# Decoding both weights in turn, with 512 tokens instead of 256 taken through float32 at the start of a fused attention and expert kernel

## The chip, the cores and the metric

The kernel runs on one core of one Trainium2 chip. The metric is the device time of one execution in microseconds (us), the median of several runs. The engines are TensorE (PE, matmuls; PEld is its weight load), VectorE (DVE), ScalarE (ACT), GpSimd (POOL) and SyncE (SP, which issues most DMAs, in program order).

## What is computed

Eight batches of 512 tokens and 32 state rows, 512 features in 8 heads of 64, go through an attention between tokens and states in both directions; the 4608 resulting rows go through a dense squared-ReLU layer (2048 wide), and then through 8 experts (1024 wide), of which each row takes one.

```python
scores = scale * x @ state.T ; a = softmax(scores) ; xread = a @ state
scores2 = scale * state @ x.T ; a2 = softmax(scores2) ; sread = a2 @ x
x = concat([xread, sread])            # 4608 rows of 512
g = relu(x @ w_in) ** 2 ; y = g @ w_out
e = argmax(cos(y, expert_emb))        # one expert a row
out = gate * (relu(y @ w1[e]) @ w2[e])
```

The two weights w_in (512x2048) and w_out (2048x512) arrive as float64; the kernel has to make float32 out of their bits before it can use them. The error allowed is small, so a product in 16 bits is made as three float16 matmuls (high by high, high by low, low by high halves); a float32 product needs no split.

## The kernel before, in words

**Order of the work.** The kernel is one program, written out by a small list scheduler in Python (`Plan`, lines 97 to 167): each piece of work is a generator that yields the engine and the estimated time that it wants next; the scheduler lets the piece go first that can start earliest, and of several with the same start the one with the lower priority number. What comes out is a fixed order of instructions on each engine. Priorities stand at the top (`PRIO_WI` and so on) and where threads are added (lines 1691 to 1707).

**Weights.** Each weight is 8 blocks of 1 MB of float64 (256 columns of w_in, or 256 rows of w_out). `block` (line 725) asks for a block into a raw place, `to_f32` (line 738) decodes it: one ACT instruction (line 759), then DVE lines 762, 764 and 775, each over 128x1024. `wi_scale` (786) takes the largest column norm of a w_in block: ACT square (792), four matmuls (799), a DVE reduction (803) and four tiny DVE instructions. `wi_block` (810) then splits the decoded block into float16 halves `wi_h` (ACT, 818) and `wi_l` (DVE, `split_lo`, line 305). All of w_in comes first, then w_out: `wo_square` (827) squares a block on ACT, and after the eighth `weights` (853) makes the scale of w_out and `wo_split` (876) splits its blocks (ACT 885, DVE 305).

**Attention.** `attention` (432) takes batch b: sums of squares on ACT (444), scales on DVE, then the products of state and tokens (625, 495), a softmax, and two transposing DMAs into `aT` (533). `state_side` (608) does the other direction; it ends in matmuls 667 to 669. `state_w` (540) multiplies the batch's state by w_in, in four parts k of 512 columns, each of 24 small float16 matmuls (561, 64 rows by 32 columns, in two row groups and four column groups), and splits the result into `sw` (ACT 566, DVE 305). So the first product of the dense layer is done as (attention weights) x (state x w_in).

**Dense layer.** `up1` (1188) goes over units u of 256 tokens, 17 in all, and over 8 chunks c of 256 hidden columns: 12 matmuls each (1210 to 1212), then `hidden` (1155) on ACT and DVE: ReLU (1166), square, and a split into `g_h`, `g_l`. For u = 0 the square is kept in float32 (`g32`, 1170); for u = 1 both the high half (1177) and the square (1179) are made on ACT; for later u DVE casts (1182). DVE subtracts (1184). `down1` (1227) multiplies by w_out: for u = 0 in float32 straight from the decoded blocks (1272, two tiles of 128 tokens side by side, 8 steps q), for u >= 1 in float16, 96 matmuls a unit (1294 to 1296). `up1` for u >= 2 waits for the down product of unit u-2, and chunk by chunk for that of u-1. `route_tile` (1030) takes each finished tile of 128 rows out of PSUM (two such places, `d_slots`): ACT square (1037), four tiny DVE instructions, ACT (310) and DVE (305) split; for the tiles of u = 0 it first waits for the scale of w_out.

**Experts.** `experts` (909) rewrites the 32 MB of expert weights as scaled float16 halves, in the gaps that ACT and DVE have beside the dense layer: squares (963), then splits into `he`, written back by DMA. It uses three places for raw halves until the attention is over. When it is done, SP loads each expert's weights (1510) and the second half of the kernel starts (`up2`, line 1586, matmuls 1604 to 1606; `down2`, 1629).

## Time and profile before

| | |
|---|---|
| median of 3 runs | 1111.26 us (1108.6 to 1115.41) |
| the profiled execution's own time | 1114.48 us |
| its span, first to last instruction | 1112.6 us |
| TensorE busy | 1030.8 us (93%) |
| DVE, ACT busy | 702.4 us (63%), 575.4 us (52%) |
| mean granted TensorE clock | 0.977 |

A window row gives, for a stretch of the span, how long each engine was busy in it and (in brackets) how many instructions that were, then the granted TensorE clock as a share of 2.4 GHz, the busy share of the DMA engines and their GB/s. A timeline row gives start, duration, engine, line, operation, what it writes and reads, sizes, and how many alike were merged. A matmul's duration includes its way through the array; back-to-back matmuls start closer together than that. A row of groups gives count, busy time, mean ns of one, and the idle time before them with what ended it.

### The profile page before, as it was taken

What the parts mean: (1) busy time and instruction counts of PE and PEld (TensorE: products, weight loads), DVE (VectorE), ACT (ScalarE), POOL (GpSimd) and SP (SyncE); (2) the same over time, 40 slices, a digit from 0 to 9 for tenths busy, and PEclk for the clock granted to TensorE, in tenths of its full rate; (3) what the DMA queues carried; (4) which work ended last, traced back from release to release, by engine and by line L of the source; (5) the groups of instructions that cost most, each with busy time, mean ns of one, the idle gap of its engine ahead of it and who ended that gap; (6) DMA issues with size and microseconds to landing.
All of it is one profiled execution on the core that took longest, in us unless ns stands there. A gap on an engine that the chain in (4) does not pass through costs nothing. (4 is left out here: it accounts for less than half of the span.)

```text
span 1112.6 us, 26342 instructions
## 1 busy us (share of the span) xinstructions
PE 1030.8 (93%) x10655; PEld 666.7 (60%) x10655; DVE 702.4 (63%) x1831; ACT 575.4 (52%) x949; POOL 128.7 (12%) x149
## 2 busy tenths in 40 slices
PE   3279789999999999999999999899999999999998
PEld 2135456555556565555555666477776767777674
DVE  6997788868888869897698777365322223222222
ACT  5678977786878777677777676210111101011110
POOL 0200000200201002001001020312121211212101
PEclk9589999999999999999999999999999999999999
DMA  8546354783668746766658487962796776594691
GB/s 291 193 156 208 100 130 123 208 219 110 169 197 186 221 150 157 216 164 189 209 115 250 132 258 222 345 140 70 250 293 155 208 227 206 159 295 135 179 299 78
DMA packets 160543, 211.74 MB, mean 190 GB/s; under 512 B 112225, under 2 KB 113505, under 8 KB 155170
## 3 DMA queue, kind: packets, MB, share of 16 engines
q1 hardware_dynamic: 152098, 182.94, 57.2%
q0 software_dynamic: 8320, 27.08, 7.7%
q8 instruction: 85, 1.39, 0.5%
q14 instruction: 40, 0.33, 0.1%
HBM read 257.92 MB, written 51.68 MB: 278 GB/s over the span
## 5 line engine op out<-in xcount | busy, mean ns | idle before, releaser
L1560 ACT ACTIVATE r<-u 128x512 f32<-128x512 f32 x70 | 41.8, 597 | 332.6 <-PE u L1606 322.0
L1294 PE MATMUL d<-wo_t,g 128*128 128x512 f16 x512 | 194.3, 380 | 3.2 <-DVE rec L305 1.9
L1296 PE MATMUL d<-wo_t,g 128*128 128x512 f16 x512 | 194.1, 379 | 0.7 <-DVE g L1184 0.6
L1295 PE MATMUL d<-wo_t,g 128*128 128x512 f16 x512 | 194.2, 379 | 0.0
L1210 PE MATMUL u<-aT,sw 128*128 128x256 f16 x512 | 140.6, 275 | 16.6 <-ACT r L1166 13.8
L1212 PE MATMUL u<-aT,sw 128*128 128x256 f16 x512 | 140.4, 274 | 0.0
L1211 PE MATMUL u<-aT,sw 128*128 128x256 f16 x512 | 140.3, 274 | 0.0
L1563 DVE CAST hh<-r 128x512 f16<-128x512 f32 x70 | 29.9, 427 | 141.8 <-ACT r L1560 140.3
L1166 ACT ACTIVATE r<-u,cg 128x512 f32<-128x512 f32 x128 | 87.2, 683 | 58.5 <-PE u L1212 36.5
L1139 POOL DMA_INDIRECT rec_d<-rec,pi x34 | 38.9, 1143 | 564.8 <-DVE g L1184 145.8
L1574 DVE TENSOR_SCALAR o<-d,rec,wo_t 128x512 f32<-128x512 f32 x35 | 28.3, 810 | 106.6 <-PE d L1629 103.1
L1184 DVE TENSOR_TENSOR g<-r,g 128x512 f16<-128x512 f32 x128 | 87.6, 687 | 1.8 <-ACT r L1179 0.4
L1629 PEld LDWEIGHTS <-hh 128*128 128x128 f16 (+1 forms) x688 | 54.5, 102 | 56.5 <-issue 0.4
L1296 PEld LDWEIGHTS <-g 128*128 128x128 f16 x512 | 50.1, 98 | 62.2 <-DVE g L1184 2.3
L1294 PEld LDWEIGHTS <-g 128*128 128x128 f16 x512 | 50.3, 98 | 50.7 <-DVE g L1182 2.3
L1179 ACT ACTIVATE r<-r 128x512 f32<-128x512 f32 x128 | 79.9, 627 | 1.5
L1295 PEld LDWEIGHTS <-g 128*128 128x128 f16 x512 | 50.1, 98 | 49.3 <-issue 2.3
L1604 PE MATMUL u<-xes,stage 128*128 128x128 f16 x448 | 78.0, 222 | 0.7 <-issue 0.7
L1605 PE MATMUL u<-xes,stage 128*128 128x128 f16 x448 | 78.0, 222 | 0.0
L1606 PE MATMUL u<-xes,stage 128*128 128x128 f16 x448 | 78.0, 222 | 0.0
L1604 PE MATMUL u<-xes,xx 128*128 128x128 f16 x416 | 70.6, 219 | 0.5 <-DMA xes<-rec 0.5
L1606 PE MATMUL u<-xes,xx 128*128 128x128 f16 x416 | 70.5, 219 | 0.0
(334 smaller groups left out, 2609.0 us busy)
## 6 DMA issues: line engine op xcount, KB each, us to landing
w_d<-he SPq DMA_DIRECT2D x128, 256.0 KB
g<-w_d SPq DMA_DIRECT2D x16, 2048.0 KB
wo_t<-w_d SPq DMA_DIRECT2D x16, 2048.0 KB
stage<-w_d SPq DMA_DIRECT2D x14, 2048.0 KB
he<-w_d SPq DMA_DIRECT2D x14, 2048.0 KB
xx<-w_d SPq DMA_DIRECT2D x13, 2048.0 KB
sw<-w_d SPq DMA_DIRECT2D x13, 2048.0 KB
stage<-in_w_dram SPq DMA_DIRECT2D x20, 1024.0 KB
```

What stands on the lines that cost most here:

```text
L1166: nc.scalar.activation(out=r, in_=ps, func=AF.Relu, scale=cg[:, g:g + 1] if u else cgq[:, c:c + 1])
L1179: nc.scalar.activation(out=r, in_=r, func=AF.Square)
L1184: V.tensor_tensor(out=gl, in0=r, in1=gh, op=ALU.subtract)
L1210: mm(o, lhsT=hl[:, i, 0, fs], rhs=aT[:, i, :], start=i == 0, stop=False)
L1211: mm(o, lhsT=hl[:, i, 0, fs], rhs=aT[:, 2 + i, :], start=False, stop=False)
L1212: mm(o, lhsT=hl[:, i, 1, fs], rhs=aT[:, i, :], start=False, stop=i == 1)
L1294: mm(ps, lhsT=g_h[:, f, ts], rhs=w[:, 0, :], start=f == 0, stop=False)
L1295: mm(ps, lhsT=g_h[:, f, ts], rhs=w[:, 1, :], start=False, stop=False)
L1296: mm(ps, lhsT=g_l[:, f, ts], rhs=w[:, 0, :], start=False, stop=f == KF - 1)
L1604: mm(p[:, j, xs], lhsT=w[:, 0, k, fs], rhs=xe[:, k, xs], start=k == 0, stop=False)
L1605: mm(p[:, j, xs], lhsT=w[:, 0, k, fs], rhs=xe[:, 4 + k, xs], start=False, stop=False)
L1606: mm(p[:, j, xs], lhsT=w[:, 1, k, fs], rhs=xe[:, k, xs], start=False, stop=k == 3)
```

## The change

- The blocks come in the order of `BLOCKS`: two of w_in, two of w_out, in turn, instead of all of w_in first. Raw places are named per block (`RAW_IN`); eight blocks have a free place at once, and the other eight take turns in four places, each freed when the block in it has been decoded and squared (`freed`).
- Decoded w_in lies in float32 (`wi32`) in the place of the next block's halves (w_in's halves are one tile `wi_t` now), and is split later (`wi_split`, priority 1.3), in order, after the float32 product has read it.
- Batch 0's state product (`first_state_w`) is made in float32 from `wi32`, eight matmuls of 256 columns for each block, as soon as two blocks of w_in are decoded; the scale of each block is put on when the result is split into `sw`. The scale of w_in is computed for two blocks at a time.
- `F32U = 2`: units u = 0 and u = 1 (512 tokens, four tiles) go through w_out in float32. Their chunks of `up1` alternate by k; `down1` does u = 0, all q, then u = 1, all q. The tiles of both wait in `route_tile` for the scale of w_out. w_out is split (priority 1.6 instead of 0.5) after the last w_in split, and block q after u = 1's product has read block q-2.
- `hidden` for u >= 2 lets ACT make the high half where DVE's planned queue is longer than ACT's by over 1 us (`Plan.load`), otherwise DVE.
- Expert halves have two raw places at first, a third (`third`) when w_out is split; fetching of experts waits for the last raw blocks and no longer for the split of w_out.
- The loader of tokens waits for block 9 of the new order instead of block 11 of the old; `group_unscale` waits for the scale of w_out; `switch` has priority 2.1 instead of 2.5.

```diff
+BLOCKS = [(kind, 2 * k + i) for k in range(NB // 2) for kind in "io" for i in range(2)]
+RAW_IN = ('g0', 'g2', 'stage0', 'stage1', 'g1', 'g3', 'phl', 'wo8', 'stage0', 'stage1', 'phl', 'wo8', 'stage0', 'stage1',
+          'phl', 'stage0')
+F32U = 2
+PRIO_SPLIT = 1.3
...
+    def load(self, eng):
+        waiting = [r for th in self.threads if isinstance(r := th[3], tuple) and r[0] == eng and th[2] <= self.free[eng]]
+        return self.free[eng] + sum(r[1] for r in waiting)
...
+    wi32 = [(wi_t[:, q + 1].rearrange("p h k f -> p (h k f)") if q < NB - 1 else
+             wo[0].rearrange("p a k d -> p (a k d)")).bitcast(F32).rearrange("p (k f) -> p k f", k=4) for q in range(NB)]
...
+    def first_state_w(stf):
+        at = plan.now()
+        for k in range(4):
+            yield sw_slots
...
+            for q in (2 * k, 2 * k + 1):
+                yield ev("wi32", q)
+            yield s_slots
...
+            for j in range(2):
+                yield "pe", 0.6
+                for c in range(4):
+                    for i in range(2):
+                        p = slice(64 * i, 64 * i + 64)
+                        mm(Sp[32 * c:32 * c + 32, i, j, :], lhsT=stf[p, c, 32 * i:32 * i + 32], rhs=wi32[2 * k + j][p, c, :],
+                           start=True, stop=True)
+            ev("wi32 read", k).set()
...
+            yield ev("swi", 2 * k + 1)
...
-    stage_slots, phl_slots, pjk_slots = Slots(plan, 3), Slots(plan, 2), Slots(plan, 1)
+    stage_slots, phl_slots, pjk_slots = Slots(plan, 2), Slots(plan, 2), Slots(plan, 1)
...
+    def block(n):
+        kind, q = BLOCKS[n]
...
+        plan.add((wi_block if kind == "i" else wo_block)(n, q), PRIO_W + 0.02 * n)
...
+    def wi_split(q):
         yield ev("swi", q)
+        yield ev("wi32 read", q // 2)
+        if q:
+            yield ev("wi", q - 1)
...
     def wo_split(q):
-        yield ev("f32", q)
         if q:
             yield ev("wo hi", q - 1)
+        else:
+            yield ev("wi", NB - 1)
         if q > 1:
             yield ev("wo", q - 2)
-            yield ev("down32", q - 2)
+            yield ev("down32", F32U - 1, q - 2)
...
     def route_tile(i, ps, k_h, rc, st):
-        if i < 2:
+        if i < 2 * F32U:
             yield ev("wo scale")
...
     def hidden(u, c, ps, k_h):
-        if u == 1:
+        early = plan.load("dve") > plan.load("act") + EASE
+        if early:
             yield act(512)
             nc.scalar.activation(out=gh, in_=r, func=AF.Square)
...
     def up1():
+        order = [(u, c) for k in range(4) for u in range(F32U) for c in (2 * k, 2 * k + 1)]
+        order += [(u, c) for u in range(F32U, NU) for c in range(8)]
...
     def down1():
+        for u in range(F32U):
+            pair = []
+            for i in range(2):
+                pair.append((yield from begin(2 * u + i)))
+            for q in range(NB):
+                yield ev("f32", q)
+                yield ev("g", u, q)
+                yield pe(16, 512)
+                for i in range(2):
+                    for f in range(2):
+                        mm(pair[i][0], lhsT=g32[:, i, 2 * q + f, 128 * u:128 * u + 128], rhs=wo32[q][:, f, :],
+                           start=q + f == 0, stop=q == NB - 1 and f == 1)
...
+            for i in range(2):
+                end(2 * u + i, *pair[i])
```

## Rows read from the trace of the kernel before

**Rows 1.** Busy time of the engines over the span, from the page

```profile
PE 1030.8 (93%) x10655; PEld 666.7 (60%) x10655; DVE 702.4 (63%) x1831; ACT 575.4 (52%) x949; POOL 128.7 (12%) x149
```

**Rows 2.** Windows of the first 167 us: busy time of each engine, clock, DMA

```profile
0.00:40.00 40.00, 12.61 (x71) 7.16 (x72) 29.06 (x57) 24.71 (x28) 1.41 (x11) 0.85 0.87 316
40.00:63.90 23.90, 5.53 (x52) 1.97 (x52) 22.43 (x49) 14.36 (x14) 5.89 (x6) 0.50 0.46 132
63.90:109.30 45.40, 44.54 (x284) 25.04 (x277) 37.97 (x54) 39.73 (x64) 0.00 (x0) 0.98 0.51 172
109.30:126.20 16.90, 10.31 (x80) 8.18 (x80) 15.47 (x55) 15.23 (x28) 0.00 (x0) 0.92 0.21 69
126.20:157.30 31.10, 30.22 (x304) 14.39 (x302) 23.27 (x51) 22.81 (x42) 0.00 (x0) 0.99 0.45 91
157.30:167.10 9.80, 7.01 (x60) 5.84 (x60) 8.54 (x14) 9.80 (x16) 0.00 (x0) 1.00 0.84 251
167.10:600.00 432.90, 422.47 (x3823) 252.67 (x3822) 357.56 (x966) 331.33 (x571) 36.16 (x48) 1.00 0.64 175
600.00:718.00 118.00, 117.27 (x796) 71.98 (x794) 80.22 (x270) 74.03 (x119) 16.57 (x18) 1.00 0.77 251
```

**Rows 3.** What PE waited for most in the first 64 us: total, times, longest

```profile
PE u L799 <- DVE wv L803: 19.7, 3, 11.1
```

**Rows 4.** DVE timeline, 77 to 84 us: the three decoding steps, two blocks each

```profile
77.91 1.28 DVE L762 TENSOR_SCALAR stage<-stage 128x1024 int32<-128x1024 int32 x2
79.11 2.35 DVE L764 SCALAR_TENSOR_TENSOR stage<-stage 128x1024 int32<-128x1024 int32 x2
...
81.85 2.37 DVE L775 SCALAR_TENSOR_TENSOR wo_t<-stage 128x1024 int32<-128x1024 int32 x2
```

**Rows 5.** DVE groups by form, first 100 us: splits of the state product and of w_in

```profile
L305 DVE SCALAR_TENSOR_TENSOR sw<-S,sw 128x512 f16<-128x512 f32 x8 | 5.5, 686 | 1.6 <-ACT sw L566 1.6
L305 DVE SCALAR_TENSOR_TENSOR wi_l<-g,swi,wi_h 128x1024 f16<-128x1024 f32 x4 | 5.1, 1284 | 2.8 <-ACT wi_h L818 2.8
```

**Rows 6.** PE timeline: state product, a float32 down step, up products, a float16 down step

```profile
67.37 0.41 PE L561 MATMUL S<-wi_h,sth 64*32 64x512 f16 x8
...
68.14 0.28 PE L1210 MATMUL u<-aT,sw 128*128 128x256 f16 x1
...
89.19 3.60 PE L1272 MATMUL d<-wo_t,g 128*128 128x512 f32 x8
92.62 0.27 PE L1210 MATMUL u<-aT,sw 128*128 128x256 f16 x1
...
93.28 3.60 PE L1272 MATMUL d<-wo_t,g 128*128 128x512 f32 x8
...
127.00 0.38 PE L1296 MATMUL d<-wo_t,g 128*128 128x512 f16 x1
...
128.94 0.38 PE L1296 MATMUL d<-wo_t,g 128*128 128x512 f16 x1
```

**Rows 7.** PE timeline: two float32 products in two column groups

```profile
16.89 1.45 PE L625 MATMUL t<-xx,stt 128*64 128x512 f32 x4 [0.27 <-issue]
```

**Rows 8.** SP timeline: first transposing DMAs, first load of experts' weights

```profile
35.15 6.79 SPq L533 DMA_TRANSPOSE aT<-xx  x2
...
693.69 0.36 SPq L1510 DMA_DIRECT2D stage<-w_d  x1
```

**Rows 9.** ACT and DVE timelines: a finished tile taken out of PSUM; last expert split

```profile
681.53 0.60 ACT L1037 ACTIVATE rec<-d 128x512 bf16<-128x512 f32 x1 [0.16 <-PE d L1296]
...
684.50 0.75 DVE L305 SCALAR_TENSOR_TENSOR rec<-d,s,rec 128x512 f16<-128x512 f32 x1
...
689.90 1.29 DVE L305 SCALAR_TENSOR_TENSOR he<-stage,se,he 128x1024 f16<-128x1024 f32 x1 [2.39 <-ACT he L310]
```

**Rows 10.** Windows: PE almost idle, and PE nearly filled, at the start

```profile
42.00:54.00 12.00, 2.82 (x12) 1.50 (x12) 10.98 (x24) 6.93 (x8) 5.89 (x6) 0.50 0.15 32
...
69.00:75.00 6.00, 5.27 (x39) 2.20 (x39) 5.04 (x7) 5.76 (x11) 0.00 (x0) 1.00 0.04 15
```

More of the change, by code (lines that the diff above doesn't have):

```diff
@@ L355, in moe_kernel @@
     iswi = const.tile([128, NB], F32, name="iswi")
-    ends = const.tile([128, 4], F32, name="ends")
+    ends = const.tile([128, 8], F32, name="ends")
+    unit = ends[:, 4:5]
     smin, ismin = ends[:, 0:2], ends[:, 2:4]
@@ L422, in loader @@
     def loader():
-        yield ev("w_in asked")
-        yield ev("raw", NB + 3)
+        yield ev("raw", LOADER)
         yield from load_x(0, 1)
@@ L743, in to_f32 @@
             plan.add(squares(w), plan.cur[1])
-            if dst is None:
-                return w
-            if q >= NB + 2:
-                yield ev("read", NB + (q - NB - 2) // 2)
+            for m in over:
+                yield ev("read", m)
             yield dve2(1024)
             V.tensor_copy(dst, w)
-            ev("f32", q - NB).set()
-            yield ev("wosq", q - NB)
-            ev("read", q).set()
-            return dst
-        raw = raw.rearrange("p (n two) -> p n two", two=2)
@@ L786, in wi_scale, with freed @@
+        plan.add(freed(n, slots, squared), plan.cur[1])
+    def freed(n, slots, squared):
+        yield squared
+        ev("read", n).set()
+        slots.release()
+    wv = {}
     def wi_scale(q, w):
@@ L835, in wo_square, with wo_block, weights @@
         ev("wosq", q).set()
-    def wo_block(q):
-        yield ev("raw", NB + q)
-        dst = wo[q + 2].rearrange("p a k d -> p (a k d)").bitcast(F32)
-        yield from to_f32(NB + q, dst, lambda a: wo_square(q, a))
-    def first_scales():
+    def wo_block(n, q):
+        yield ev("raw", n)
+        yield from to_f32(n, wo32[q].rearrange("p k d -> p (k d)"), lambda a: wo_square(q, a), ev("wosq", q))
+        ev("f32", q).set()
+    def weights():
+        for n in range(1, len(BLOCKS)):
+            yield from block(n)
+            if n == LOADER:
+                ev("w_in asked").set()
@@ L844, in first_scales @@
         for q in range(NB):
+            yield ev("wosq", q)
             yield ev("swi", q)
[L846 to L847 removed]
+        yield tiny(2)
         V.tensor_reduce(out=smin[:, 0:1], in_=swi, axis=X, op=ALU.min)
         V.tensor_reduce(out=ismin[:, 0:1], in_=iswi, axis=X, op=ALU.max)
[L850 to L865 removed]
@@ L924, in put, with third @@
                 stage_slots.release()
+        def third():
+            yield ev("wo", NB - 1)
+            yield ev("down32", F32U - 1, NB - 1)
+            put(last)
         def more():
@@ L970, in experts @@
         plan.add(fetch(), PRIO_E)
+        plan.add(third(), PRIO_E)
         plan.add(more(), PRIO_E)
@@ L1179, in hidden @@
         nc.scalar.activation(out=r, in_=r, func=AF.Square)
-        if u > 1:
+        if not early:
             yield dve2(512)
@@ new lines, in up1 @@
+        order = [(u, c) for k in range(4) for u in range(F32U) for c in (2 * k, 2 * k + 1)]
+        order += [(u, c) for u in range(F32U, NU) for c in range(8)]
+        for u, c in order:
+            if c == 0:
+                if u > 1:
+                    yield ev("down", u - 2, 7)
+                yield ev("xg", u)
+            if u < 2 * B:
+                yield ev("sw", u // 2, c // 2)
+            if u > 1 and c:
+                yield ev("down", u - 1, c - 1)
+            at = plan.now()
+            yield u_slots
+            plan.cur[2] = max(at, plan.now())
+            ps, k_h = ps_u.tile([128, 512], F32, name="u").rearrange("p (f t) -> p f t", f=2), u_slots.last()
+            for ff in range(2):
+                o = ps[:, ff, :]
+                if u < 2 * B:
+                    (hl, k_s), (aT, k_a) = sw[u // 2, c // 2], xg[u]
+                    fs = slice((2 * c + ff) % 4 * 128, (2 * c + ff) % 4 * 128 + 128)
+                    yield pe(6, 256)
+                    for i in range(2):
+                        mm(o, lhsT=hl[:, i, 0, fs], rhs=aT[:, i, :], start=i == 0, stop=False)
+                        mm(o, lhsT=hl[:, i, 0, fs], rhs=aT[:, 2 + i, :], start=False, stop=False)
+                        mm(o, lhsT=hl[:, i, 1, fs], rhs=aT[:, i, :], start=False, stop=i == 1)
+                else:
+                    yield pe(12, 256)
+                    for k in range(4):
+                        wh, wl = (wi_t[:, c, h, k, ff * 128:ff * 128 + 128] for h in range(2))
+                        mm(o, lhsT=wh, rhs=x8_h[:, k, :], start=k == 0, stop=False)
+                        mm(o, lhsT=wh, rhs=x8_l[:, k, :], start=False, stop=False)
+                        mm(o, lhsT=wl, rhs=x8_h[:, k, :], start=False, stop=k == 3)
+            if u < 2 * B and u % 2 and c % 2:
+                sw_slots.release(k_s)
+            plan.add(hidden(u, c, ps, k_h), 0)
+            if c == 7:
+                if u < 2 * B:
+                    aT_slots.release(k_a)
+                ev("up", u).set()
@@ L1691, in start @@
     def start():
-        yield from block(0, wiv[:, :, 0:BW * WS], BW)
-        plan.add(wi_block(0), PRIO_WI)
+        yield from block(0)
         yield from load_x(0, 0)
```

282 lines of the change are left out of this document (121 added, 161 removed).

## Prediction

> **What bounds the kernel now.** I read the page's busy shares first: PE is busy 93% of the span, no other engine over 63% [rows 1]. So PE's idle time is what an edit can win, and the windows say where it lies [rows 2]. From 167.1 to 718 us PE is idle 11.2 us of 550.9 (432.9 - 422.47 and 118 - 117.27), while in the first 167.1 us it is idle 56.9: 27.4 up to 40 us, 18.4 from 40 to 63.9, 0.9, 6.6, 0.9 and 2.8 in the stretches after. In 40 to 63.9 DVE is busy 22.43 of 23.9 us, and PE's longest waits up to there end at DVE: 19.7 us at the column norms of w_in (L803) [rows 3]. DVE there decodes w_in and splits it, and only then can the first product of the dense layer start, at 63.9 us. Its data from the attention had been asked for much sooner: the first two transposing DMAs were issued from 35.15 on [rows 8]. The mark that I use below is 167.1 us, where up(2) is done and down(2) begins (u in brackets). Up to there all weight work is in; after it the program is the same in both kernels and PE-bound, so what is won by then should reach the end.
>
> **Part 1, the float32 state product and w_in's later split: the start moves from 63.9 to about 42 us.** Before the first up product, the old order decodes all eight w_in blocks and splits them. The new one needs two. A block costs DVE (1.28 + 2.35 + 2.37) / 2 = 3.0 us [rows 4], so two blocks are ready soon after 20 us, and the product and its split (0.69 us on DVE for each half, [rows 5]) do not come last any more. Last come the two transposing DMAs of the attention weights, issued from 35.15 to 41.94 [rows 8]; when they land the rows do not show. I take 42 us, the end of the issue; bounds 38.5 (half the issue, the first of the two) and 49 (the issue once more behind it: in 0 to 40 us the DMA engines are busy 0.87 of the time [rows 2], and the new order asks for eight raw blocks at once). The product itself is 64 matmuls of 256 columns in float32 where before there were 96 of 512 in float16. Before, a part of 24 takes 67.37 to 68.14 = 0.77 us, 3.1 for four [rows 6]. A float32 down step of eight instructions takes 3.43 us (89.19 to 92.62), 0.43 per instruction of 512 columns and two instructions per matmul [rows 6]. Half the columns and all eight tiles at once make 0.43 us a block, 3.4 in all, +0.3. The trace has no float32 product in eight tiles. The nearest is one in two column groups: four instructions, two matmuls, in 1.45 us [rows 7], less than the 1.71 that four would take in turn, so they overlap. Bounds: 3.1 and 27.4 (eight tiles in turn); I take 3.4, nearest to the float16 row in the same tiles.
>
> **Part 2, unit 1's down product in float32: +6.7 us on PE.** Nine float16 matmuls take 128.94 - 127.00 = 1.94 us, 0.216 each, so 96 take 20.7; eight float32 steps of 3.43 take 27.4 [rows 6]. Nothing hides this. What it buys: ACT's second square and DVE's eight subtractions for unit 1 go, and w_out's split need not stand before unit 1. Those were the 6.6 us of idle PE in 109.3 to 126.2 [rows 2].
>
> **Part 3, how fast weights feed PE.** PE's work from the first up product until down(0) is done: up(0), up(1) 16 chunks of 12 products at 0.11 (six in 92.62 to 93.28, [rows 6]) 21; down(0) 27.4; three remaining state parts 2.6; norms, state side of batch 0, scores of batch 1 some 6 (estimate): 57. From 42 that ends at 99 if it is fed. DVE: until 109.3 it is busy 29.1 + 22.4 + 38.0 = 89.5 us [rows 2]. The new order takes the eight w_in splits (10.2, [rows 5]) and the five w_out splits of that stretch (6.4) out from before the last block, and lets batch 1's attention (priority 1.15 against 1.16 and more for blocks 8 to 15) come in: four passes at 1.2, two splits at 1.28, two at 0.69, small ones 3: about 12. So 85 us of DVE. DVE was idle 10.9 us in the first 40 and 6% after [rows 2]; 85 busy us end at about 100, and the last w_out step follows: down(0) ends at 104, 5 us after what PE alone would need. Bounds 99 (PE alone) and 119 (w_in's splits and batch 1's state split, 15 us, also in front).
>
> **Part 4, between down(0) and down(1).** Both tiles of unit 0 end together, there are two PSUM places, and down(1) needs them back. Behind the wait stands PE's next down product, and everything in program order after it. Taking a tile out lasts 681.53 to 685.25 = 3.7 us [rows 9]; I take 4 idle (bounds 0, if batch 1's state product fills it, and 6, the second tile).
>
> **Part 5, the rest to the mark.** Down(1) 27.4, batch 1's state product 3.1 and scores 3, up(2) 10.5: 44. Meanwhile DVE must split w_in (10.2), w_out (10.2), the state product (5.5) and take out four tiles: some 35 us of 44, so it fits, narrowly. The 2.8 us that up(2) waited at its end [rows 2] should shrink, as it now runs beside down(1); 0.5 left. The casts of `hidden` by load, and two raw places for experts instead of three until the split of w_out is done, cost nothing while DVE and ACT have the gaps that rows 2 show (DVE 357.6 of 432.9, ACT 331.3); bounds -3 to +3. The shorter queue of SP work before the start is neutral: same blocks, same bytes.
>
> **Sum.** 104 + 4 + 44 + 0.5 = 152.5 against 167.1: 14.6 us earlier. In the profiled execution that is 1114.48 - 14.6 = 1099.9; it lay 3.2 above the median of 1111.26, so against the median 1096.7, say **1097**. Its own range: start 39 to 46, feeding 0 to 8, gap 0 to 6, rest -3 to +3, not all at one end: 1087 to 1105.
>
> **Rivals.**
> *Experts bound the second half* (chance 0.13). The last expert split ends at 691.2 and the first load of expert weights is issued at 693.7, three more 2 MB loads behind it (estimate: 698) [rows 8, 9]; 2 MB at the 251 GB/s of that stretch [rows 2] take 8, so the expert half could start at 706 where it starts at 718. If the expert pieces do not move with the dense layer (two raw places, a later start), only 12 us can be won, and if they slip by 6, 6: 1105. Against: they fill gaps, and gaps move along.
> *Decoding ends no earlier* (0.12). If the scheduler puts w_in's splits before the last blocks, down(0) ends at 114 and 10 of the 14.6 are gone: 1107. For: such splits are ready early. Against: at equal start the blocks come first.
> *The clock* (slower; 0.08). In 42 to 54 us PE is busy 2.8 of 12 us and its granted clock is 0.50, the lower level; in 69 to 75 it is busy 5.3 of 6 and the clock is 1.00 [rows 10]. In the new build-up PE works between waits for DVE from 42 to 104. If half of its 57 us ran at 1.2 GHz it would need 28 more: 1111.3 - 14.6 + 28 = 1125. From 15 us of work at the lower level on, the change is a loss. Against: 57 of 62 us is as full as the stretch with 1.00. The Trainium skill, "TensorE: Matmul & The Clock Gate" (section on HAM oscillation), says that bursts of matmuls with idle gaps between them fall back to the halved clock again and again; that rule is this rival, and both windows of rows 10 agree with it.
> *Float32 tiles in turn* (0.05). The state product then takes 27.4 us, some 24 more, of which the feeding slack takes 5: 1116.
> *Fed without gaps* (0.10). Start 40, no feeding loss, no gap at the tiles: 40 + 57 + 44 = 141, 26 earlier, 1085, less a part that later waits give back: 1088.
>
> **How the numbers follow.** The forecast keeps 0.52. This kernel's runs differ by 0.3% either way, so about 1%, 11.1 us, is what counts as a change: below 1100.1 is faster. The forecast's own range lies two thirds below that line (0.36), the fed case wholly (0.10), the first two rivals with a third (0.08), and I round up for the later idle time that might also shrink: faster 0.57. Slower than 1122.4 are the clock and part of the tiles in turn, with a little for a stall that I do not see: 0.11. Same 0.32. The range must take in the two rivals at 1105 and 1107 and the fed case: 1086 to 1111.
>
> **What would show it.** Right: first up product at 38 to 46 us; no float16 state product of batch 0; 128 float32 down instructions, at 0.43 apart; granted clock 1.00 from about 46 on; down(2) begins at 145 to 160; PE idle before it 35 to 45 us instead of 57; the same distance from there to the end. Wrong: up products waiting for the transposing DMA beyond 50; DVE decoding the last w_out block after 110; clock 0.5 in the build-up; an idle PE near 700 with SP's first weight loads just before it.

## The result and the profile after

The changed kernel takes **1099.53 us** (median of 8 runs, 1097.84 to 1102.71) where the kernel before takes 1108.7 (8 runs, 1107.36 to 1115.41): a ratio of 0.9905 over the runs, 95% interval 0.9884 to 0.9927; the medians lie 9.2 us apart. The prediction was 1097 us and "faster" at 0.57. The gain is smaller than the 14.6 us of the sum, and half of it came from another place than the sum said.

The two profiled executions differ by more, 1114.48 and 1097.84. Between 5 and 6 us of that is no gain: from the second expert down product to the end the code is the same, and the profiled run of before needed 1112.6 - 748.2 = 364.4 us there, the one after 358.6. Experiment 8, the old code with other priorities, needed 359.2. So I compare the profiled pair only up to there.

Windows of the changed kernel (columns as in [rows 2]): the start, up to the end of down(0), the gap, down(1), and the rest up to the mark where down(2) begins:

```profile
0.00:43.50 43.50, 14.78 (x87) 9.04 (x88) 30.09 (x54) 26.05 (x31) 2.04 (x11) 0.74 0.84 297
43.50:118.70 75.20, 65.13 (x469) 36.51 (x470) 59.95 (x109) 58.72 (x90) 0.78 (x6) 0.88 0.50 158
118.70:121.60 2.90, 2.16 (x18) 1.25 (x18) 2.52 (x15) 2.17 (x5) 0.00 (x0) 1.00 0.00 0
121.60:155.00 33.40, 33.38 (x204) 16.22 (x205) 30.87 (x62) 24.01 (x35) 0.00 (x0) 1.00 0.27 48
155.00:161.30 6.30, 6.18 (x92) 5.54 (x89) 4.13 (x16) 5.61 (x12) 0.00 (x0) 1.00 0.89 325
```

The first up product starts at 43.5 instead of 63.9, but the mark lies at 161.3 instead of 167.1: of the 20 us that the start gives, 6 are left. PE is idle 39.7 us up to the mark (the five rows), 56.9 before [rows 2]; in exchange it works 121.6 instead of 110.2 us.

Where the other 14.6 us went shows when both kernels are counted from their first up product to the mark. That takes 117.8 us now, 103.2 before. PE's idle time in it is nearly the same (10.9 and 11.1 us); its work grew from 92.1 to 106.9 us. Of this, 6.7 are the float32 product of unit 1 (Part 2 of the prediction), some 5 a lower clock (below), and the other 3 about what PE no longer does ahead of the first up product (14.8 us of work there now, 18.1 before).

What PE waited for up to the mark, after (total, times, longest):

```profile
PE u L844 <- ACT pjk L836: 28.9, 4, 10.2
PE u L1271 <- DMA aT<-xx: 3.4, 1, 3.4
...
PE d L1334 <- DVE rec L315: 0.8, 1, 0.8
```

The transposing DMA ends the wait for the first up product, as the prediction's part 1 said; the step from down(0) to down(1) costs 0.8 us. Of the 28.9 us that column norms wait for ACT, 20.9 lie ahead of the first up product, where the kernel before waited for DVE [rows 3]; the other 8.00 are new. PE timeline around that wait:

```profile
68.43 0.66 PE L576 MATMUL S<-wi,sthl 64*32 64x256 f32 x16
69.02 0.61 PE L844 MATMUL u<-pjk,oneb 128*128 128x256 bf16 x4
...
70.83 3.60 PE L1334 MATMUL d<-wo_t,g 128*128 128x512 f32 x8
...
76.32 0.60 PE L844 MATMUL u<-pjk,oneb 128*128 128x256 bf16 x4
84.92 1.01 PE L844 MATMUL u<-pjk,oneb 128*128 128x256 bf16 x4 [8.00 <-ACT pjk L836]
...
88.13 1.11 PE L576 MATMUL S<-wi,sthl 64*32 64x256 f32 x16
88.99 1.10 PE L576 MATMUL S<-wo_t,sthl 64*32 64x256 f32 x16
```

PE's next instruction at 76.9 is the column norm of w_in's block 6, and it waits 8.00 us for that block's square. ACT's timeline over the same time:

```profile
69.91 1.16 ACT L836 ACTIVATE pjk<-stage 128x1024 bf16<-128x1024 f32 x1
...
78.72 1.21 ACT L892 ACTIVATE pjk<-he 128x1024 bf16<-128x1024 f32 x1
...
79.84 1.13 ACT L458 ACTIVATE xx<-xx 128x1024 bf16<-128x1024 f32 x1
...
83.61 1.26 ACT L836 ACTIVATE pjk<-stage 128x1024 bf16<-128x1024 f32 x1
```

Block 5's square lies in the one `pjk` buffer from 69.91 until PE has read it, and PE does so only at 76.32, behind a float32 down step of 3.6 us and the state side. So w_out's squares, which use the same buffer, start at 78.72; ACT works without a pause through the whole hole (8.00 of 8.00 us below), with the squares of batch 1's attention (L458) in between, and block 6's square comes at 83.61. PE's clock is down in two spells, right after the start and behind the hole:

```profile
43.50:48.30 4.80, 4.78 (x34) 2.58 (x34) 1.33 (x6) 1.97 (x4) 0.73 (x6) 0.50 0.74 142
...
76.90:84.90 8.00, 0.02 (x1) 0.00 (x0) 7.21 (x13) 8.00 (x14) 0.00 (x0) 0.64 0.49 190
84.90:92.60 7.70, 7.20 (x56) 3.87 (x56) 4.69 (x16) 3.07 (x5) 0.00 (x0) 0.50 0.42 138
92.60:161.30 68.70, 66.86 (x469) 36.73 (x468) 58.01 (x131) 55.90 (x87) 0.00 (x0) 1.00 0.34 101
```

In both spells the granted clock is 0.50, the lower of the two levels 1.2 and 2.4 GHz, although PE is busy 4.78 of 4.80 and 7.20 of 7.70 us. Ahead of the first, PE had worked only 1.0 us of the 8.5 since 35.0; ahead of the second, 0.02 of 8.00. A float32 state block takes 0.86 us from start to start at the lower level (88.13 to 88.99) instead of 0.59 (68.43 to 69.02). If the 12.0 busy us had been half as long at the full clock, the two spells cost 2.4 and 3.6, together 6.0 us; this is an estimate and rather high, since the state block is less than twice as long. The like estimate for the kernel before, 63.9 to 69.0 (busy 5.10 us, clock 0.85), is 0.8. And from the end of the hole to the mark PE is idle only 2.3 of 76.4 us (the last two rows), so in that stretch no other engine holds it up much.

DVE's timeline around the last decoded block (stage; its second and third step, lines 812 and 819):

```profile
99.26 1.22 DVE L812 SCALAR_TENSOR_TENSOR stage<-stage 128x1024 int32<-128x1024 int32 x1
100.39 1.28 DVE L315 SCALAR_TENSOR_TENSOR wi<-wi,swi 128x1024 f16<-128x1024 f32 x1
101.59 1.28 DVE L315 SCALAR_TENSOR_TENSOR xx<-xx,sx 128x1024 f16<-128x1024 f32 x1
103.07 1.28 DVE L315 SCALAR_TENSOR_TENSOR xx<-xx,sx 128x1024 f16<-128x1024 f32 x1 [0.20 <-ACT xx L329]
104.27 1.28 DVE L315 SCALAR_TENSOR_TENSOR wi<-wi,swi 128x1024 f16<-128x1024 f32 x1
...
105.61 1.22 DVE L819 SCALAR_TENSOR_TENSOR wo_t<-stage 128x1024 int32<-128x1024 int32 x1
```

Between its second and its third step DVE does two splits of w_in and two of batch 1's attention, 5 us of work for later. The last block is decoded from 105.6 to 106.8, and down(0) ends at 118.7. PE did not stand still for this block: it is busy nearly all the time from 84.9 on.

**The second half of the gain** lies 550 us further on. The rows of the tiles w_d (the experts' splits stored), d and hh (the down products of the dense layer and of the experts) give count, min/median/max in ns, then the first and last start. Before:

```profile
L327 SPq DMA_DIRECT2D w_d<-he x128: 332/386/1546, 156.8 to 691.2; - x128
L1296 PE MATMUL d<-wo_t,g x512: 377/379/390, 127.0 to 717.8; 128*128 128x512 f16 x171
L1629 PE MATMUL d<-he,hh x224: 376/379/389, 736.4 to 1106.7; 128*128 128x512 f16 x112
```

and after:

```profile
L337 SPq DMA_DIRECT2D w_d<-he x128: 332/344/1545, 166.5 to 670.2; - x128
L1357 PE MATMUL d<-wo_t,g x480: 377/379/390, 161.7 to 713.1; 128*128 128x512 f16 x160
L1690 PE MATMUL d<-he,hh x224: 376/379/389, 726.8 to 1090.2; 128*128 128x512 f16 x112
```

The last expert split is stored 21.0 us earlier. From the dense layer's last product to the first expert down product it takes 726.8 - 713.1 = 13.7 us instead of 18.6. So 9.6 us are won when the experts' products begin: 4.7 at the end of the dense layer and 4.9 behind it. PE does the same 218 matmul instructions behind it in both kernels. Windows of before:

```profile
700.00:718.80 18.80, 18.07 (x100) 8.71 (x97) 6.72 (x31) 2.93 (x6) 10.54 (x11) 1.00 1.02 364
717.80:736.40 18.60, 14.14 (x218) 13.57 (x217) 7.46 (x34) 3.38 (x7) 0.00 (x0) 0.82 0.97 199
722.70:727.70 5.00, 4.96 (x57) 4.96 (x57) 0.87 (x2) 0.58 (x1) 0.00 (x0) 0.51 1.00 367
```

and of after:

```profile
690.00:705.00 15.00, 14.46 (x108) 9.27 (x107) 10.12 (x54) 5.50 (x10) 4.14 (x4) 1.00 0.32 95
713.10:726.80 13.70, 11.63 (x218) 11.34 (x217) 5.21 (x16) 3.17 (x6) 0.00 (x0) 1.00 0.95 249
```

The 4.9 us are 2.4 of idle time (4.46 before, 2.07 after) and 2.5 of busy time, at the lower clock (0.51 from 722.7 to 727.7) behind one wait of 3.93 us. That wait is not for expert weights. Timelines of before, around a tile finished at the end of the dense layer (`rec`), which the routing needs transposed (`xr`):

```profile
704.39 1.06 POOL L1530 DMA_INDIRECT rec<-rec_d,wo_t  x1 [48.74 <-PE u L1219]
710.00 0.75 DVE L305 SCALAR_TENSOR_TENSOR rec<-d,s,rec 128x512 f16<-128x512 f32 x1 [0.82 <-issue]
713.05 1.27 SPq L1550 DMA_TRANSPOSE xes<-rec  x1
714.38 2.35 SPq L1051 DMA_TRANSPOSE xr<-rec  x1
722.74 0.19 PE L1060 MATMUL t<-en_h,xr 128*128 128x8 f16 x1 [3.93 <-DMA xr<-rec]
```

and of after:

```profile
699.68 1.07 POOL L1591 DMA_INDIRECT rec<-rec_d,wo_t  x1 [47.92 <-PE t L1175]
703.23 1.26 SPq L1611 DMA_TRANSPOSE xes<-rec  x1
706.79 0.75 DVE L315 SCALAR_TENSOR_TENSOR rec<-d,s,rec 128x512 f16<-128x512 f32 x1 [0.82 <-issue]
707.57 1.23 SPq L1109 DMA_TRANSPOSE xr<-rec  x1
```

Before, the loads of expert weights issued from 693.69 [rows 8] keep the DMA engines full from 700 to 718.8 (share 1.02). The first gather of tokens for the experts (L1530) starts at 704.39 amid them, and SP, which works in program order, waits until 713.05 to transpose what it brings (`xes`), 8.7 us later. The finished tile is ready at 710.75, but its transposing DMA stands behind that one and goes out 3.6 us late, at 714.38. After, the loads are issued 21 us earlier, the share from 690 to 705 is 0.32, gather and transpose are 3.6 us apart, and the tile's transposing DMA goes out as soon as the tile is ready. So late splits make late loads, and these hold up the routing. That the full DMA engines are what makes the gather slow is read from these rows; no run moved that gather alone. Experiments 7 and 8 move the splits.

### The profile page after: what moved, and what is told of

It reads as the page before. It is cut to its first block, busy times and chain, and to the rows that moved or that the text cites. A ratio compares the mean times of both kernels' runs of the same rounds, so it can differ in the third digit from the quotient of the medians.

```text
span 1096.1 us, 26333 instructions
## 1 busy us (share of the span) xinstructions
PE 1038.3 (95%) x10655; PEld 670.9 (61%) x10655; DVE 680.7 (62%) x1771; ACT 592.9 (54%) x982; POOL 123.1 (11%) x149
## 5 line engine op out<-in xcount | busy, mean ns | idle before, releaser
L1355 PE MATMUL d<-wo_t,g 128*128 128x512 f16 x480 | 181.9, 379 | 0.2 <-DVE f L1099 0.2
L1357 PE MATMUL d<-wo_t,g 128*128 128x512 f16 x480 | 181.9, 379 | 0.1
L1356 PE MATMUL d<-wo_t,g 128*128 128x512 f16 x480 | 181.9, 379 | 0.0
L1271 PE MATMUL u<-aT,sw 128*128 128x256 f16 x512 | 141.4, 276 | 11.1 <-ACT r L1224 7.3
L1224 ACT ACTIVATE r<-u,cg 128x512 f32<-128x512 f32 x120 | 81.7, 682 | 38.4 <-PE u L1273 20.7
L1243 DVE TENSOR_TENSOR g<-r,g 128x512 f16<-128x512 f32 x120 | 82.5, 688 | 7.4 <-ACT r L1238 5.7
L1357 PEld LDWEIGHTS <-g 128*128 128x128 f16 x480 | 47.0, 98 | 57.1 <-DVE g L1243 0.6
L1666 PE MATMUL u<-xes,stage 128*128 128x128 f16 x448 | 75.9, 219 | 0.0
L1667 PE MATMUL u<-xes,stage 128*128 128x128 f16 x448 | 75.9, 219 | 0.0
L1665 PE MATMUL u<-xes,stage 128*128 128x128 f16 x448 | 75.9, 219 | 0.0
L1238 ACT ACTIVATE r<-r 128x512 f32<-128x512 f32 x120 | 74.7, 626 | 1.4
L1355 PEld LDWEIGHTS <-g 128*128 128x128 f16 x480 | 47.2, 98 | 44.8 <-issue 0.5
L1356 PEld LDWEIGHTS <-g 128*128 128x128 f16 x480 | 46.9, 98 | 44.6 <-issue 0.4
```

Of the source, the lines that this page charges most:

```text
L1224: nc.scalar.activation(out=r, in_=ps, func=AF.Relu, scale=cg[:, g:g + 1] if u >= F32U else cgq[:, c:c + 1])
L1238: nc.scalar.activation(out=r, in_=r, func=AF.Square)
L1243: V.tensor_tensor(out=gl, in0=r, in1=gh, op=ALU.subtract)
L1271: mm(o, lhsT=hl[:, i, 0, fs], rhs=aT[:, i, :], start=i == 0, stop=False)
L1355: mm(ps, lhsT=g_h[:, f, ts], rhs=w[:, 0, :], start=f == 0, stop=False)
L1356: mm(ps, lhsT=g_h[:, f, ts], rhs=w[:, 1, :], start=False, stop=False)
```

## The experiments

Twelve kernels ran, in four comparisons; each ratio is to the kernel before in the same comparison (medians 1110.3, 1109.6, 1118.8 and 1111.2 us), and the changed kernel's own is 0.9905. The times in this table are read as above: the mark, the last expert split stored, the last dense down product, the first expert down product, and the distance between these two.

| kernel | mark | last split | dense ends | experts begin | distance | ratio (95%) |
|---|---|---|---|---|---|---|
| before | 167.1 | 691.2 | 717.8 | 736.4 | 18.6 | 1 |
| changed | 161.3 | 670.2 | 713.1 | 726.8 | 13.7 | 0.9905 (0.9884 to 0.9927) |
| 1 own buffers for squares | 161.0 | 694.2 | 710.4 | 744.2 | 33.8 | 1.0032 (1.0013 to 1.0052) |
| 2 unit 1 in float16 | 167.7 | 686.2 | 717.4 | 730.2 | 12.8 | 0.9923 (0.9897 to 0.9948) |
| 3 state product in float16 | 165.7 | 688.9 | 716.9 | 733.5 | 16.6 | 0.9972 (0.9952 to 0.9991) |
| 4 `switch` at 2.5 | 161.1 | 673.1 | 715.9 | 729.6 | 13.7 | 0.9919 (0.9898 to 0.9939) |
| 5 w_in splits, batch 1 later | 160.7 | 688.1 | 721.6 | 732.4 | 10.8 | 0.9982 (0.9957 to 1.0007) |
| 6 batch 1 later | 175.9 | 675.6 | 726.9 | 741.7 | 14.8 | 1.0026 (1.0007 to 1.0045) |
| 7 experts later | 161.9 | 711.4 | 714.4 | 744.1 | 29.7 | 1.0073 (1.0047 to 1.0099) |
| 8 before, experts earlier | 169.6 | 675.2 | 722.4 | 733.9 | 11.5 | 0.9970 (0.9948 to 0.9991) |
| 9 no casts by load | 162.5 | 730.3 | 723.7 | 775.6 | 51.9 | 1.0285 (1.0256 to 1.0314) |
| 10 experts at 1.4 | 162.8 | 672.0 | 721.5 | 735.7 | 14.2 | 0.9955 (0.9933 to 0.9977) |
| 11 w_in splits later | 161.3 | 691.8 | 708.1 | 742.2 | 34.1 | 1.0028 (1.0006 to 1.0049) |
| 12 as 11, experts at 1.9 | 162.3 | 638.6 | 746.0 | 753.6 | 7.6 | 1.0143 (1.0109 to 1.0177) |

**Experiment 1: the squares of w_in in two buffers of their own.**

```diff
+    sq_slots = Slots(plan, 2)
...
-        yield pjk_slots
+        yield sq_slots
...
-        sq = att.tile([128, 4, BW], BF16, name="pjk")
+        sq = wo[1][:, q % 2].bitcast(BF16).rearrange("p k d -> p (k d)").rearrange("p (k f) -> p k f", k=4)
```

> The changed kernel, with two buffers of their own for the squares of w_in blocks (in the still unused place of w_out's second split) where they shared one with the squares of w_out. Theory (one square buffer held block 5's square until PE got to its norm matmuls, so block 6's square came late and PE stood 8.0 us before block 6's norm matmuls, with the lower clock behind it): the 8 us hole shrinks to under 3 us, down(2) begins at 150 to 156 instead of 161.3, and the time is 1089 to 1095. Rival (ACT was busy 8.10 of the 8.10 us of the hole and is the limit there, whatever the buffer): the hole only moves, 1098 to 1101.

The hole shrank from 8.00 to 4.74 us, but new gaps opened (1.54 us at 83.3, 1.87 at 120.1), and the mark stayed at 161.0. The last block was decoded at 105.8, as in the changed kernel. Part of the effect is hidden by the start: the first up product came at 45.2, where the changed kernel had 43.5 (experiments 7, 9 and 10, with nothing edited up to there, had 44.9 to 45.2). Counted from there the mark comes after 115.8 us instead of 117.8, and 1.1 of the difference is idle time. So the buffer is worth about 2 us at the mark, not the 5 to 11 of the theory. And the total was lost at another place: the dense layer ended 2.7 us earlier, the experts began 17.4 us later. That was not foreseen by either theory, and the runs from 7 on look at it.

**Experiment 2: unit 1 in float16 again.**

```diff
-F32U = 2
+F32U = 1
```

> The changed kernel with F32U = 1: only 256 tokens go through w_out in float32, unit 1 in float16 halves as before the change. Theory (the 6.7 us that float32 costs on PE buy more than that, since float16 would wait for the splits of both weights, some 20 us of DVE after the last block): 1103 to 1110, with PE idle between down(0) and down(1) for 8 us or more. Rival (PE work is what counts and DVE would have split in time): 1092 to 1096.

The mark moved to 167.7: unit 1 in float32 is worth 6.4 us there (4.8 when counted from the first up product, at 45.1 in this run), although its product takes 6.7 us longer on PE. PE was idle 7.0 of the 20.1 us between the two down products, near the 8 of the theory. In the time it is worth less than can be measured (0.9923 against 0.9905, the intervals overlap), neither what the theory nor what the rival gave.

**Experiment 3: batch 0's state product in float16 from split w_in.** This needs the splits early, so their priority goes with it.

```diff
-PRIO_SPLIT = 1.3
+PRIO_SPLIT = 1.0
...
-            plan.add(first_state_w(stf), 0.6)
+        plan.add(state_w(b, sth, stl), PRIO_SW if b else 1.1)
...
-        yield ev("wi32 read", q // 2)
```

> The changed kernel with batch 0's state product again from float16 halves, so each pair of w_in blocks is split (DVE 1.28 and ACT 1.15 us a block) before it; the splits have priority 1.0. All else as changed. Theory (the start of the first up product hangs on the transposing DMA, not on the weights, but the four later parts each wait for splits): first up product still at 43 to 46 us, down(2) 4 to 10 us later than 161.3, 1103 to 1110. Rival (the splits have to be done by DVE at some time before the mark anyway, and moving them costs nothing): 1098 to 1101.

The mark moved to 165.7, 4.4 us later, and 0.67% of the ratio was lost (7.4 us), as the theory said. But not in the way it said: the first up product came at 47.8 us, not at 43 to 46, and from there to the mark it took as long as in the changed kernel (117.9 and 117.8 us). So the float32 state product is worth its 4 us at the start, where the splits of the first blocks would stand ahead.

**Experiment 4: `switch` back at its old priority.**

```diff
-        plan.add(switch(), 2.1)
+        plan.add(switch(), 2.5)
```

> The changed kernel with the priority of the thread that builds the experts' lists back at 2.5 (2.1 in the change). Before and after differ by 4.7 us where the dense layer ends, and by 9.6 where the first expert product through w2 begins. Theory (the earlier lists make that difference, about 5 us): 1103 to 1106. Rival (the difference comes from where the last tiles' transposes fall, which has nothing to do with that priority): 1098 to 1101.

The distance stays at 13.7, the ratio is the same within its interval. The rival held: this edit isn't where the 4.9 us come from.

**Experiment 5: the splits of w_in and batch 1's attention behind the last block.**

```diff
-PRIO_SPLIT = 1.3
+PRIO_SPLIT = 1.6
...
-            plan.add(attention(b), PRIO_A0 if b == 0 else 1.15 if b == 1 else PRIO_A1)
+            plan.add(attention(b), PRIO_A0 if b == 0 else 1.5 if b == 1 else PRIO_A1)
```

> The changed kernel with the split of w_in at priority 1.6 instead of 1.3 and batch 1's attention at 1.5 instead of 1.15, so that both stand behind the last weight block. Theory (work of later use stands ahead of the last blocks on DVE and ACT): the last decoding instruction of w_out starts at 95 to 100 us instead of 105.6, down(0) ends at 108 to 113 instead of 118.7, the 8.0 us hole at 76.9 is under 4, and down(2) begins at 155 to 158 instead of 161.3; median 1093 to 1098. Rival (the work is only displaced, DVE and ACT are as full behind the last block as ahead of it): down(0) ends earlier, but down(1) or the second up products wait for it, down(2) begins within 1.5 us of 161.3; median 1098 to 1102.

The last block was decoded at 97.3, 8.3 us earlier, and down(0) ended at 114.6, 4.1 earlier; the hole was still 6.89 us, and down(2) began at 160.7. The rival held: what was put off was late next. The total was worse than it said, since the dense layer ended 8.5 us later.

**Experiment 6: batch 1's attention alone.** Edit: the second half of the diff above.

> The changed kernel with batch 1's attention alone at priority 1.5 instead of 1.15; the split of w_in stays at 1.3. Theory (the attention's squares on ACT are what makes the square of w_in's block 6 late): the hole at 76.9 shrinks from 8.0 to under 5 us, down(0) ends 4 to 8 us before 118.7, down(2) begins at 157 to 160; median 1095 to 1099. Rival (batch 1's attention is needed soon after, by up(2)): hole shorter, but up(2) waits for the transposed attention and down(2) begins at 161 or later; median 1099 to 1104.

The hole was 6.88 us, down(0) ended 1.1 us earlier, and then up(2) waited 8.9 us for the transposing DMA of batch 1, with down(2) at 175.9. The rival's mechanism held, at a higher price (1114.0 us).

**Experiment 7: the experts' pieces last, once the attention is done.**

```diff
-PRIO_E1 = 2.2
+PRIO_E1 = 6
```

> The changed kernel with the experts' pieces at priority 6 instead of 2.2 once the attention is done, nothing else. Theory (how early the experts' splits are done sets how long PE needs from the end of the dense layer to the first expert down product: 18.7 us before, 13.8 after, with the last split stored at 691 and 670 us): the last store moves from 670 to 676 or later, the distance grows to 15 to 20 us and the median to 1101 to 1106. Rival (the distance comes from the routing, not from the splits): distance 13 to 14.5 us, median 1098 to 1101.

Mark and dense layer stayed within 1.3 us; the last split moved by 41 us and the distance from 13.7 to 29.7. The theory held, with a larger price than expected (1117.6 us). PE's longest wait from 700 on in this run:

```profile
PE u L1665 <- DMA stage<-w_d: 11.2, 1, 11.2
```

It is for a load of expert weights, which can't start until the splits are stored.

**Experiment 8: the kernel before, with the experts' pieces earlier.**

```diff
-PRIO_E = 4
-PRIO_E1 = 2.2
+PRIO_E = 2.2
+PRIO_E1 = 1.4
```

> The kernel before with the experts' pieces at priority 2.2 instead of 4, and 1.4 instead of 2.2 once the attention is done; nothing of the change. Theory (as for the run with the experts later): the last split is stored at 668 to 682 us instead of 691, the distance from the end of the dense layer to the first expert down product falls from 18.7 to 13 to 16 us, median 1103 to 1107 against 1108.7. Rival (the distance comes from the routing): last store earlier, distance 18 to 19 us, median 1107.5 to 1112, or more if the pieces push aside the dense layer's own work.

Without anything of the change, the last split is stored at 675.2 and the distance falls to 11.5, further than the 13 to 16 of the theory. PE has no idle time in these 11.5 us, its clock is 1.00 in them, and the first gather and its transpose are 3.4 us apart. The dense layer pays 4.6 us for it (2.5 of them are a later start, already there at the mark), and 0.3% are won. So in the kernel before it was the late splits of the experts that held up the second half.

**Experiment 9: no casts by load.**

```diff
-        early = plan.load("dve") > plan.load("act") + EASE
+        early = False
```

> The changed kernel without the casts by load: in hidden the cast stays where it was, whatever DVE and ACT have queued. Theory (these casts take work from DVE beside the dense layer, 437.8 us busy before and 425.3 after, and so let the experts' splits end at 670 instead of 691 us): down(2) still begins within 2 us of 161.3, but the last split is stored at 685 us or later, the distance from the end of the dense layer to the first expert down product grows from 13.8 to 17 us or more, and the median is 1104 to 1118. Rival (the casts cost and give nothing, as predicted; the splits end early because the weights are in sooner): last store at 665 to 678, distance 13 to 15 us, median 1098 to 1101.

The theory held, and far beyond its numbers: the mark at 162.5, the last split at 730.3, the distance 51.9, and a ratio of 1.0285. DVE's casts between 161 and 700 us, in the groups of the changed kernel and then of this one (count, busy us, mean ns, idle before):

```profile
L1241 DVE CAST g<-r 128x512 f16<-128x512 f32 x76 | 32.2, 424 | 28.3 <-ACT r L1238 28.1
```

```profile
L1241 DVE CAST g<-r 128x512 f16<-128x512 f32 x117 | 49.9, 428 | 31.5 <-ACT r L1238 31.0
```

42 of 118 casts are ACT's in the changed kernel, 26.4 us of them, and DVE has 17.7 us less. What this buys is not DVE's time as such: in experiment 9 both engines stand idle for over 120 of the 539 us from 161 to 700 (DVE busy 418.3, ACT 396.0; before 436.5 and 408.5, with five more splits done by then), and yet the splits end 39 us later than before. It is behind early: 14 stores by 250 us, where before and the changed kernel both have 21. Why it falls that far behind the kernel before is open. The two raw places instead of three and the later split of w_out are left as candidates; neither was undone alone.

**Experiment 10: the experts' pieces at 1.4 in the changed kernel.** Edit as the second half of experiment 8's.

> The changed kernel with the experts' pieces at priority 1.4 instead of 2.2 once the attention is done (the opposite of the run at 6). Theory (the distance follows the end of the splits): last store 2 to 8 us before 670, distance 11 to 13.5 instead of 13.8, median 1096 to 1099 if the dense layer does not get longer. Rival (at 670 the splits are no longer what comes last): distance 13.5 to 14.2, median 1098.5 to 1102.

Neither held as a whole: the last split did not come earlier (672.0), the distance is the rival's (14.2), and the dense layer ended 8 us later.

**Experiment 11: the splits of w_in alone later.** Edit: the first half of experiment 5's.

> The changed kernel with the split of w_in at priority 1.6 instead of 1.3 and batch 1's attention as it is. Theory (as in the run that moved both, whose last block was decoded at 97.3 instead of 105.6 us): last decoding instruction at 100 to 104, down(0) ends 1 to 4 us before 118.7; down(2) begins within 1.5 us of 161.3, since it is the sum of PE's work and one hole that sets it; median 1098 to 1106, the experts' order deciding. Rival (the last block sets it): down(2) begins 2 to 5 us earlier, median 1095 to 1098.

The last block was decoded at 104.0 and the mark stayed at 161.3, as the theory said; down(0), which it had 1 to 4 us earlier, ended at 118.8 as in the changed kernel. The dense layer ended at 708.1, the earliest of all, but the splits only at 691.8, and the experts began 15.4 us later than in the changed kernel. What PE waits for there, and SP's timeline ahead of it:

```profile
PE t L1118 <- DMA xr<-rec: 14.8, 1, 14.8
PE u L1665 <- DMA xes<-rec: 5.3, 1, 5.3
```

```profile
694.32 0.37 SPq L1571 DMA_DIRECT2D stage<-w_d  x1
...
698.27 0.34 SPq L1571 DMA_DIRECT2D xx<-w_d  x1
701.90 10.91 SPq L1109 DMA_TRANSPOSE xr<-rec  x1
```

SP issues the first three loads of expert weights, 2 MB each, as soon as the splits are stored; the routing's transposing DMA right behind them holds SP for 10.91 us. In the changed kernel the same three loads are spread over 11 us (below), and the transposing DMA at 707.57 comes 24 us behind them and takes 1.23:

```profile
672.72 0.38 SPq L1571 DMA_DIRECT2D stage<-w_d  x1
...
683.79 0.35 SPq L1571 DMA_DIRECT2D xx<-w_d  x1
```

**Experiment 12: as 11, with the experts' pieces at 1.9 throughout.** It was meant to beat both kernels.

```diff
-PRIO_SPLIT = 1.3
+PRIO_SPLIT = 1.6
...
-PRIO_E = 4
-PRIO_E1 = 2.2
+PRIO_E = 1.9
+PRIO_E1 = 1.9
```

> The changed kernel with the split of w_in at 1.6 (as in the run before, whose dense layer ended at 708.0 us but whose last expert split was stored only at 691.8) and the experts' pieces at 1.9 throughout. Theory (PE starts the first expert down product at the later of two times: the end of the dense layer plus 11 to 14 us, and the last store of an expert split plus 44 to 50 us): last store at 650 to 672, so that the dense layer's end decides; it ends at 708 to 716, the first expert down product starts 11 to 15 us behind it, ratio to the kernel before 0.985 to 0.993. Rival (the pieces that come earlier push the dense layer's own work aside, as in the kernel before with the experts earlier, whose dense layer ended 4.6 us later): dense layer ends at 717 or later, ratio 0.994 to 1.000.

The rival held, and more: the splits are done at 638.6, and the dense layer ends 33 us later. No version tried beats the changed kernel.

## Why the prediction was right, and where not

**What read right.** The place of the loss, DVE's work ahead of the first up product; the end of that wait by the transposing DMA (42 said, 43.5 measured); unit 1's product (128 float32 instructions; down(1) takes 33.4 us, and batch 1's work fits into it); PE's idle time up to the mark (35 to 45 said, 39.7 measured). The total time lies inside the forecast's own range, 1087 to 1105, but in part by luck: the mark came 8.8 us later than the sum had it, and 4.9 us were won behind the dense layer, where the sum had nothing. Of the signs, the mark itself (145 to 160 said, 161.3 measured) and the clock (1.00 from about 46 on) did not come.

**Part 3 failed.** Down(0) was to end at 104 and ended at 118.7; from 43.5 that is 75.2 us where the sum had 62. The step took DVE's work as one sum, 85 busy us by 100, and added 5 behind PE. The sum itself was near: DVE has worked 30.09 + 59.95 = 90.0 us when down(0) ends. But it stood idle for 28.7 us. The blocks pass ACT, DVE, ACT again and PE, with one buffer for the squares, and ACT was never priced; it is what PE's 8 us hole waits for. In PE's terms the 13.2 us are 5.1 of idle time (10.1 instead of 5), about 6 of the lower clock, and some 2 of work, such as the first of batch 1's state parts (at 102.4), that the sum had placed after down(0); the rest from down(1) on took 39.7 us instead of 44.5.

**The term that was left out is the clock.** Up to the mark the account closes. The sum had 42 us for the start, 101 of work and 9.5 idle: 152.5. Measured are 43.5, 106.9 and 10.9: 161.3. So idle time was sized nearly right in total, with more of it before down(0) and less after, and of the 8.8 us that the mark is late, 5.9 are work that took longer. The lower clock (6.0 by the estimate above) is as large as that, and the sum put it at nothing: it took the full clock from 46 us on, and it did not see that a hole of 8 us would bring the lower one back. This fits experiments 1, 5 and 11, which shorten the hole or bring the last block forward and leave the mark within 0.6 us of 161.3: each still has a hole (4.74 to 7.95 us), and behind it PE is idle only 3.3 to 4.5 of some 77 us, whatever DVE has decoded. A version without the hole, which might bring the mark to 152, was not found.

**The rival "decoding ends no earlier"** saw the order rightly: splits and batch 1's attention stand ahead of the last blocks. Its 114 for down(0) was the better number. But this order is not what held PE: experiment 5 put those pieces behind the last block and the mark moved by 0.6 us. **The clock rival** came true in part: it wanted 28.5 us of work at the lower level, 12.0 busy us were spent there, at a cost of about 6. The Trainium skill, "TensorE: Matmul & The Clock Gate" (section on HAM oscillation), describes a kernel whose every wait between bursts of matmuls brings the halved clock back; the rows of 76.9 to 92.6 agree for one such wait, 8.0 us long, and between the first up product and the mark the run has no other above 0.8.

**Part 1's product** was mis-sized a little: eight float32 tiles at once take 0.59 us a block instead of 0.43, so 4.7 us for eight at the full clock and not 3.4. Tiles in turn (27.4) is excluded.

**Part 4** gave 4 us of idle PE; it was 0.76, since up products and batch 1's scores fill the gap.

**Part 5 held two errors that cancelled in part.** "The same distance from the mark to the end" is wrong: 4.9 us more were won behind the dense layer. And "the casts of `hidden` by load cost nothing" is the term that was off most: in this kernel they are worth 3.8% (1.0285 against 0.9905), about 42 us. That is their worth in this kernel only: the one before has none of them and its splits end at 691.2, and experiment 9 shows the rest of the change without them, with the splits 39 us later than that. The reason given was that DVE and ACT have gaps. They have, but a piece of expert work needs ACT, then DVE, then a store, in the order that the scheduler wrote, and that chain ended last. The rival on the experts saw the right chain and read its slack with the wrong sign: it let PE start its experts at 706, 12 us before the dense layer ends. It priced one load of 2 MB (8 us); three follow one another, the DMA engines are full until 718.8, and the routing's own DMAs have to pass among them. The rows of before [rows 8, 9] give the last split at 691 but not what follows it; in the seven kernels where the splits are late (before, 1, 2, 3, 5, 9 and 11) 44.0 to 50.4 us pass from the last store to the first expert down product, with loads and the routing's transposing DMAs in one queue. Where the splits end by 676 (the changed kernel, 4, 6, 8, 10), the dense layer decides, 11.5 to 14.8 us after its end; 2 and 5, with 12.8 and 10.8, fit this reading about as well. Experiments 7 (32.7 us from the store) and 12 (7.6 after the dense layer) lie outside both bands. So the bands are what these runs show, and no rule. By them, and by experiment 8, 736.4 was set by the splits in the kernel before, 4 to 7 us later than the dense layer alone would have it (717.8 and 11.5 to 14.8), and the change took that away.

By medians, then: some 5 us from the earlier start and the float32 products, and some 5 from the experts' splits, together 9.2.

## What to carry to other kernels

Price a pipeline by the engine that hands over last in each step, and by its single buffers, and not by one engine's sum: DVE's sum was right within 5 us, and the hole came from ACT. Price the clock behind every pause of PE: here idle time was sized within 1.5 us, and about 6 us were lost because the work behind two pauses ran at the lower level. Where a later stage starts at the later of two chains, find which one ends last by moving one of them (here by priority) before an edit is costed at nothing; an edit that changes only who does a cast can be the largest of all. And read a window by its counterpart in a second run before a difference of 5 us in unchanged code is taken for a gain, and count it from an event inside the run: the first up product alone moved by 1.7 us between runs of the same code.

## What the hardware showed that was not expected

- Behind a pause PE was busy nearly without a break and still had the lower clock (0.50 to 0.51): 4.78 of 4.8 us from the first up product on, 7.20 of 7.7 behind the hole, 4.96 of 5.0 from 722.7 on in the kernel before.
- A gather of tokens amid full DMA engines was usable after 8.7 us (kernel before, share 1.02), where it took 3.6 with a share of 0.32.
- A transposing DMA behind three loads of 2 MB holds SP for 10.91 us, where such a one takes 1.23 in a quiet stretch (707.57 in the changed kernel); one issued 5.3 us behind the second of two such loads took 1.31 there (at 680.46).
- Small float32 matmuls (64 rows by 32 columns) do run side by side: 16 instructions in 0.59 us, 0.037 each, where half of a 512-column instruction's 0.43 would be 0.21 each in turn.
- The expert half of the same code differs by run and not by kernel: 358.3 to 360.3 us in the changed kernel, experiments 1 to 8 and 12, but 364.4 in the profiled run of before and 364.6 to 368.4 in experiments 9 to 11, whose comparison had a kernel before of 1118.8 us. PE's waits there are short ones without a releaser in the trace. The cause is open.
